# Half of a layer's first matrix product by Strassen's scheme, in a fused windowed-attention and MLP kernel

## The chip, the cores and the metric

The kernel runs on one core of one Trainium2 chip. The metric is device time in microseconds (us), the median over several runs; lower is better. The core has five engines that run beside each other, each with an in-order queue of its own: TensorE (PE in the profile; PEld is its weight load), VectorE (DVE), ScalarE (ACT), GpSimd (POOL) and SyncE (SP), which here only issues DMAs.

## The reference

Attention over a window with four sink positions, then a layer norm and an MLP with a residual. The draw gives 4 batches, 8 heads, 768 positions, head size 64, so 3072 rows of 512 columns go into the MLP, whose hidden width is 2048.

```python
scores = scale * q @ k.T                      # per batch and head, scale = 1/sqrt(64)
keep = (pos_k < 4) | ((pos_q - pos_k >= 0) & (pos_q - pos_k < 128))
a = softmax(where(keep, scores, -1e9))
x = (a @ v).transpose(0, 2, 1, 3).reshape(B, S, H * D)
xn = (x - mean(x)) / sqrt(var(x) + 1e-6) * g_ln
out = x + maximum(xn @ w_ch1, 0.0) @ w_ch2    # w_ch1: 512x2048, w_ch2: 2048x512
```

## The kernel before

**Tiling.** The 3072 rows are 12 chunks (`NC`) of 256 rows, three to a batch; `c` is the chunk, `R = c % 3` its place in the batch. A chunk has two tiles `t` of 128 rows. For each chunk `chunk` loads q, k and v (DMAs from GpSimd's queue: `nat`, `vn`) and transposes q and k (DMA transposes from SP's queue: `kq`); `attend` makes the scores (TensorE into a pair of PSUM banks, L763, with the sinks of L767), their exponentials (ScalarE, L777, bf16 `pe`), and multiplies these by a band mask (VectorE, L781); `value` multiplies by v (TensorE, L800 for the sinks, L805), divides by the sums and takes the layer norm's statistics (VectorE, L818 to L826), the inverse root (GpSimd, L832 and L833), the normed rows (VectorE, L835) and transposes them by a DMA into `xnt` (L845).

**First layer.** `mlp` computes, for a chunk, 16 column groups of 128 hidden values, two to a step `u` of eight: per step 8 matmuls of 128x128 weights by 256 rows of `xnt` into one PSUM bank `ph` (L880), then a relu into `hq` (L890 on ScalarE or L892 on VectorE). For the first two chunks the matmuls stream 128 rows instead (L873).

**Second layer.** From the third chunk on, `wino` computes it with Winograd's form of Strassen's scheme: four sums of parts of the hidden values (`s1` to `s4`, VectorE, L943, `hs`), then seven products of eight matmuls (`p1`, `p2`, `p7`, `p6`, `p4`, `p5`, `p3`, L960), and VectorE instructions that combine PSUM regions and the residual (`keep`, L974; `final`, L981).

**Order.** Nothing is left to the hardware's choice: each step is an `op` with the engines that may run it, an assumed duration and a priority; `Plan.run` lays them out in a list schedule, and every engine's queue is emitted in the order of the planned starts. From priority 40 on TensorE's order is that of the priorities alone. With `T = 16c + 8`, the first layer of chunk `c` has priorities `T + 0.5 + u`, and the seven products follow 8 later; the scores of the next chunk have priority `T - 5.3` and `T - 2.0`, its value products `T + 2` and `T + 3`. Buffers come from rings: four single PSUM banks (`one`), two pairs (`pair`), 8 `hq`, 10 `hs`, 16 `x`, 12 `pe`.

Of the kernel before, what the change touches and what calls it, by code (L numbers as in the profile page):

```python
# [7 lines left out]
FP32 = mybir.dt.float32  # L8
BF16 = mybir.dt.bfloat16
# [55 lines left out]
class Plan:  # L65
# [7 lines left out]
    SHARED = 36.0  # L73

# [38 lines left out]
    def run(self):  # L113
# [8 lines left out]
        while ready:  # L122
# [50 lines left out]
            if o.dma is None:  # L173
                o.end = st + lat
            else:
                busy, first, last = o.dma
                q = "POOL" if e == "POOL" else "HW"
                at = max(st + occ + first, dma_free[q], dma_free["all"] if st < self.SHARED else 0.0) + busy
                dma_free[q] = dma_free["all"] = at
                o.end = at + last  # L180
                lanes[q][n_dma[q] % self.LANES] = o.end
                n_dma[q] += 1
# [29 lines left out]
def fix(occ, extra=0.09):  # L212
# [11 lines left out]

LOW, HIGH = 1e-9, 1e9
# [4 lines left out]
           w1p=(0.15, 1.7, 2.05, 2.8), pm=2, w2p=(4.5, 4.51, 4.52, 4.53), by_tile=2, wino=2, vp=(0.0, 0.1, 2.0, 2.1, 4.2, 4.3), ld1=0.05)  # L230
# [131 lines left out]
def kernel(  # L362
# [47 lines left out]
    ring("pe", 12, [128, 2, 512], BF16)  # L410
    ring("ps", 3, [128, 256], BF16)
    ring("kts", 2, [128, HP, 32], BF16)
    ring("x", 16, [128, DM], BF16)
# [3 lines left out]
    ring("hs", 10, [128, 2, 2, 128], BF16)  # L417
    ring("tm", 6, [128, 256], FP32)
# [101 lines left out]
    for b in range(1, B):  # L520
        P.op(f"vs{b}", {"DVE": dve(520)}, 48.0 * b - 20, lambda e, b=b: V.tensor_tensor(
            vs[b], vc[:, b, :].unsqueeze(1).to_broadcast([128, H, 65]),
            sel.unsqueeze(2).to_broadcast([128, H, 65]), op=ALU.mult),
            reads=[Bc["vcd"], Bc["vc"], Bc["sel"]], writes=[Bvs[b]], nb=40.0 * b)
# [11 lines left out]
    def at(c, step):  # L536
        return 16.0 * c - 8.0 + PAR[step]
# [17 lines left out]
    def behind(c):  # L555
        return [roots[2 * (c - 3) + 1]] if c >= PAR["behind"] else []

    def load_v(t, prio):
        b, r = t // RB, t % RB
        bv = Buf(f"v{t}", "vn")  # L560
        vn_b[t] = bv
        P.op(f"vld{t}", {"POOL": (0.87, 0.9)}, prio, lambda e: G.dma_start(  # L562
            bv.t[:, :, 0:64], v[b, :, 128 * r:128 * (r + 1), :].rearrange("h p d -> p h d")),
            writes=[bv], dma=SW, after=list(ones_of.values()) + behind(t // 2))
# [13 lines left out]
    def chunk(c):  # L578
# [54 lines left out]
        elif c < PAR["by_dma"]:  # L633
            loaded = Buf(f"l{c}")
            for i in range(2):
                load4(c, "kq"[i], (PAR["ld1"] if c == 1 else ld) + 0.01 * i, loaded)
            for hh in range(2):
                pt = Buf(f"pt{c}{hh}", "one")

                def tr(e, pt=pt, hh=hh):  # L640
                    pb = pt.t.bitcast(BF16).rearrange("p (h k i g) -> p h i k g", h=2, k=2, i=4)
                    for h in range(2):
                        for i in range(4):
                            for h2 in range(2):
                                nc.tensor.transpose(pb[64 * h2:64 * h2 + 64, h, i], n4_b[c].t[:, 4 * hh + 2 * h + h2, i, :], ident)  # L645
                P.op(f"tr{c}{hh}", pe(0.46), d + 0.02 + 0.1 * hh, tr, reads=[loaded, Bc["ident"]],
                                  hold=[n4_b[c], T], writes=[pt], mode="c")
                done = Buf(f"T{c}{hh}")
                tile_of[2 * c, hh] = tile_of[2 * c + 1, hh] = done
                evict(f"ev{c}{hh}", d + 0.05 + 0.1 * hh, 1024,  # L650
                      lambda pt=pt: pt.t.bitcast(BF16).rearrange("p (m i g) -> p m g i", m=4, i=4),
                      lambda hh=hh: T.t[:, 2 * hh:2 * hh + 2].rearrange("p h k (g i) -> p (h k) g i", i=4), [pt], [T, done], fp=True)
        else:
            for x, (nm, src) in enumerate((("k", k), ("q", q))):
                for i in range(2):
                    nat = Buf(f"{nm}n{c}{i}", "nat")
                    ap = src[b, :, 256 * R + 128 * i:256 * R + 128 * (i + 1), :].rearrange("h p d -> p h d")
                    P.op(f"{nm}ld{c}{i}", {"POOL": (0.87, 0.9)}, ld + 0.01 * i + 0.1 * x,
                         lambda e, nat=nat, ap=ap: G.dma_start(nat.t, ap), writes=[nat], dma=SW, after=behind(c))  # L659
                    P.op(f"tr{nm}{c}{i}", {"SP": (1.2, 1.2)}, d + 0.01 * i, lambda e, nat=nat, i=i, x=x: dma_t(  # L660
                        T.t[:, :, x, 128 * i:128 * i + 128], nat.t.rearrange("p h d -> p (h d)")),
                        reads=[nat], writes=[T], dma=HW_X, after=[scores[c - 1]])
# [75 lines left out]
    def attend(c):  # L738
# [6 lines left out]
        for half in range(2):  # L745
# [28 lines left out]
            for j, pp in enumerate(pps):  # L774
# [5 lines left out]
                P.op(f"mk{c}{hp}", {"DVE": dve(2 * n, 0.52)}, d + 0.2 + 0.05 * j, lambda e, pb=pb, mm=mm:  # L780
                     V.tensor_mul(pb.t[:, :, 0:n], pb.t[:, :, 0:n], mm),  # L781
                     reads=[Bc["mask" if R else "mask0"]], rw=[pb])
# [4 lines left out]
        for i in range(2):  # L787
# [3 lines left out]
            value(c, i, pes, ps, (PAR["av2"] if c == 2 else at(c, "av")) + PAR["avi"] * i, part, [2 * c + i - 1, 2 * c + i] if R or i else [2 * c])  # L791

    def value(c, i, pes, ps, d, part, srcs):
# [24 lines left out]
        P.op(f"rc{t}", {"DVE": fix(0.115)}, d + 0.1, lambda e: V.reciprocal(rc(), pv()[:, :, :, 64]),  # L818
             reads=[po], writes=[rcb])
        P.op(f"x{t}", {"DVE": dve(512)}, d + 0.11, lambda e: V.tensor_tensor(  # L820
# [3 lines left out]
        P.op(f"bn{t}", {"DVE": fix(0.60)}, d + 0.12, lambda e: V.bn_stats(st.t[:, 8:14], x.t),  # L824
             reads=[x], writes=[st, mv])
        P.op(f"ag{t}", {"DVE": fix(0.09)}, d + 0.13, lambda e: V.bn_aggr(st.t[:, 14:16], st.t[:, 8:14]),  # L826
# [4 lines left out]
        roots[t] = P.op(f"rs{t}", {"POOL": (0.83, 0.88)}, d + (0.5 if scaled else 5), lambda e: (  # L831
# [3 lines left out]
        P.op(f"xc{t}", {"DVE": fix(0.26)}, d + (0.6 if scaled else 0.14), lambda e: V.tensor_scalar(  # L835
# [8 lines left out]
        if c >= PAR["x_by_dma"]:  # L844
            P.op(f"trx{t}", {"SP": (1.2, 1.2)}, d + 0.5, lambda e: dma_t(xnt_b[c].t[:, :, 128 * i:128 * i + 128], xc.t),  # L845
                 reads=[xc], writes=[xnt_b[c]], dma=HW_X)
# [13 lines left out]

    def mlp(c):
# [5 lines left out]
        for u in range(NH1 // 2):  # L867
# [15 lines left out]
            pr = T + u + 0.5  # L883
# [9 lines left out]
            P.op(f"rl{c}_{u}", {"ACT": act(512), "DVE": dve(512)}, pr - 3, rl, reads=[ph], writes=[hb], hold=[hg])  # L893
            h1.append(hb)
        T += 8
        if c >= PAR["wino"]:
            return wino(c, T, hq, h1)
# [29 lines left out]
    def wino(c, T, hq, h1):  # L927
# [3 lines left out]
        deps = {n: [h1[4 * g + (0 if n[2] == "1" else 1)::2][:2] for g in range(2)] for n in part}  # L931
# [7 lines left out]
        for i, (n, x0, x1, op) in enumerate((("s3", "a11", "a21", ALU.subtract), ("s1", "a21", "a22", ALU.add),  # L939
                                             ("s2", "s1", "a11", ALU.subtract), ("s4", "a12", "s2", ALU.subtract))):  # L940
            for g in range(2):
                sb[n, g] = Buf(f"{n}_{c}{g}", "hs")
                P.op(f"{n}_{c}{g}", {"DVE": dve(512, 0.52)}, T - 4 + 4 * g + 0.2 * i, lambda e, n=n, x0=x0, x1=x1, g=g, op=op: V.tensor_tensor(  # L943
# [27 lines left out]
        def keep(name, r, done, half, pr):  # L971
            tm[name] = Buf(f"tm{name}{c}", "tm")
            i, sl = half // 2, slice(256 * (half % 2), 256 * (half % 2) + 256)
            return P.op(f"tm{name}_{c}", {"DVE": dve(256, 1.14)}, pr, lambda e: V.tensor_tensor(  # L974
# [3 lines left out]
        def final(r, done, name, half, pr):  # L978
            i, sl = half // 2, slice(256 * (half % 2), 256 * (half % 2) + 256)
            oo[half] = Buf(f"oo{c}{half}")  # L980
            return P.op(f"o{c}_{half}", {"DVE": dve(256, 1.14)}, pr, lambda e: V.tensor_tensor(  # L981
# [51 lines left out]
    for c in range(NC):  # L1033
        mlp(c)
# [94 lines left out]
```

## Time and profile before

| what | value |
|---|---|
| median of 3 runs | 211.38 us (210.68 to 211.71) |
| the profiled execution's own time | 211.71 us |
| its span, first to last instruction | 210.2 us |
| TensorE busy | 203.0 us, 97% |
| VectorE busy | 162.2 us, 77% |
| ScalarE busy | 114.1 us, 54% |
| GpSimd busy | 83.5 us, 40% |
| granted TensorE clock | 1.000 |

Durations in a row are of one instruction; TensorE's instructions overlap, so the pace of a stream of matmuls is read from the time a run of them takes in the chain of waits, divided by their number, and not from the mean of one. Engines that are not on the chain may idle at no cost.

### The profile page before, as it was taken

To read this page: it belongs to the slowest core of one execution; us is meant where nothing else is said; L and a number is where in the kernel's file an instruction comes from. 1 tells how busy PE (TensorE), PEld (TensorE's weight loads), DVE (VectorE), ACT (ScalarE), POOL (GpSimd) and SP (SyncE) were. 2 spreads that over 40 slices of the span, in tenths; PEclk is the share of its full clock that TensorE was granted. 3 is DMA by queue.
4 is the path that set the end of the run, shared out by engine and by line. 5 is a ranking of instruction groups with operands and counts; after the bars stand their busy time and mean duration, and the time that the engine had idled before them with its cause. 6 is when DMAs were issued, how large, how long until landed. Compare 5 with 4: busy or idle time off the path is not lost.

```text
span 210.2 us, 6259 instructions
## 1 busy us (share of the span) xinstructions
PE 203.0 (97%) x2539; PEld 167.9 (80%) x2544; DVE 162.2 (77%) x410; ACT 114.1 (54%) x168; POOL 83.5 (40%) x126
## 2 busy tenths in 40 slices
PE   6978999999999999999999999999999999999994
PEld 2657997764787997997987987987988988988883
DVE  5579759999688688798687797797787786797353
ACT  2559479837564564564556555554457457450620
POOL 7967583369058057058066066066020020020000
PEclk9999999999999999999999999999999999999999
DMA  5999999999999949939959939939954520220202
GB/s 115 156 198 191 199 191 208 189 173 154 212 167 127 172 109 136 188 78 120 166 122 150 174 79 156 172 77 151 177 100 53 150 53 3 100 50 4 103 30 83
DMA packets 101243, 27.51 MB, mean 131 GB/s; under 512 B 89556, under 2 KB 99032, under 8 KB 101208
## 3 DMA queue, kind: packets, MB, share of 16 engines
q0 software_dynamic: 67712, 13.37, 77.7%
q1 hardware_dynamic: 33208, 13.41, 35.5%
q8 instruction: 21, 0.34, 0.7%
q10 hardware_dynamic: 288, 0.26, 0.4%
q14 instruction: 14, 0.11, 0.2%
HBM read 27.30 MB, written 6.29 MB: 160 GB/s over the span
## 4 chain that ended last, share of the span: by engine, by line
PE 90%; DMA 3%; DVE 3%; POOL 2%; issue 0%; DVEq 0%
PE one L880 33%; PE one L960 30%; PE one L873 7%; PE one L911 7%; PE pair L805 5%; PE pair L763 4%; DMA n4b<-in_q_dram 3%; PE pair L800 2%; PE one L645 1%; POOL nat L599 1%; PE one L767 1%; DVE xnt L857 1%; DVE kq L568 1%; POOL vn L562 0%; DVE st L824 0%
## 5 line engine op out<-in xcount | busy, mean ns | idle before, releaser
L890 ACT ACTIVATE hq<-one 128x512 bf16<-128x512 f32 x92 | 55.0, 597 | 55.7 <-PE one L880 46.7
L880 PE MATMUL one<-xnt,w 128*128 128x256 bf16 x640 | 74.5, 273 | 0.0
L880 PEld LDWEIGHTS <-w 128*128 128x128 bf16 x640 | 61.4, 98 | 7.0
L777 ACT ACTIVATE pe<-pair 128x1024 bf16<-128x1024 f32 (+1 forms) x40 | 36.2, 960 | 23.2 <-PE pair L763 19.0
L832 POOL TENSOR_SCALAR st<-st 128x1 f32<-128x1 f32 x24 | 6.2, 259 | 88.2 <-DVE rec L818 74.6
L960 PEld LDWEIGHTS <-hs 128*128 128x128 bf16 x320 | 30.0, 98 | 5.2 <-DVE tm L974 0.3
L974 DVE TENSOR_TENSOR tm<-one,x 128x256 f32<-128x256 f32 x40 | 16.9, 422 | 12.3 <-PE one L960 12.3
L781 DVE TENSOR_TENSOR pe<-pe,mask 128x1024 bf16<-128x1024 bf16 (+1 forms) x40 | 24.9, 644 | 1.0 <-ACT pe L777 0.8
L960 PEld LDWEIGHTS <-hq 128*128 128x128 bf16 x240 | 23.5, 98 | 2.7
L562 POOL DMA_DIRECT2D vn<-in_v_dram x24 | 21.8, 922 | 2.0 <-DMA w<-in_moe_w_ch_dram 1.1
L943 DVE TENSOR_TENSOR hs<-hq 128x512 bf16<-128x512 bf16 x40 | 15.4, 413 | 5.3 <-ACT hq L890 5.2
L960 PE MATMUL one<-w,hq 128*128 128x256 bf16 x160 | 19.1, 273 | 0.0
L981 DVE TENSOR_TENSOR ot<-one,tm 128x256 f32<-128x256 f32 x40 | 16.7, 418 | 1.1 <-PE one L960 0.9
L820 DVE TENSOR_TENSOR x<-pair,rec 128x512 bf16<-128x512 f32 x24 | 16.6, 691 | 0.8
L824 DVE BATCH_NORM_STATS2 st<-x 128x6 f32<-128x512 bf16 x24 | 16.6, 692 | 0.5
L873 PE MATMUL one<-xnt,w 128*128 128x128 bf16 x256 | 16.3, 219 | 0.5 <-DVE xnt L857 0.5
L873 PEld LDWEIGHTS <-w 128*128 128x128 bf16 x256 | 14.7, 98 | 1.6 <-issue 0.5
L659 POOL DMA_DIRECT2D nat<-in_k_dram x16 | 15.0, 938 | 2.5 <-DMA w<-in_moe_w_ch_dram 2.5
L659 POOL DMA_DIRECT2D nat<-in_q_dram x16 | 14.2, 898 | 3.4 <-DMA w<-in_moe_w_ch_dram 3.4
L833 POOL TENSOR_TENSOR st<-st,mhalf 128x1 f32<-128x1 f32 x24 | 14.2, 592 | 2.0
L911 PE MATMUL one<-w,hq 128*128 128x512 bf16 x60 | 14.8, 380 | 0.2
L805 PE MATMUL pair<-vn,pe 128*128 128x65 bf16 x352 | 14.6, 193 | 0.0
(113 smaller groups left out, 245.1 us busy)
## 6 DMA issues: line engine op xcount, KB each, us to landing
out_dram<-ot SPq DMA_DIRECT2D x17, 256.0 KB
w<-in_moe_w_ch_dram POOLq DMA_DIRECT2D x8, 512.0 KB, 12.6
vn<-in_v_dram POOLq DMA_DIRECT2D x24, 128.0 KB, 7.2
nat<-in_k_dram POOLq DMA_DIRECT2D x17, 128.0 KB, 4.8
nat<-in_q_dram POOLq DMA_DIRECT2D x17, 128.0 KB, 5.3
out_dram<-ot SPq DMA_DIRECT2D x14, 128.0 KB
kq<-nat SPq DMA_TRANSPOSE x32
xnt<-xc SPq DMA_TRANSPOSE x20
```

Source lines behind the costliest of these rows:

```text
L562: P.op(f"vld{t}", {"POOL": (0.87, 0.9)}, prio, lambda e: G.dma_start(bv.t[:, :, 0:64], v[b, :, 128 * r:128 * (r + 1), :].rearrange("h p d ...
L659: lambda e, nat=nat, ap=ap: G.dma_start(nat.t, ap), writes=[nat], dma=SW, after=behind(c))
L777: P.op(f"ex{c}{hp}", {"ACT": act(2 * n)}, d + 0.1 + 0.05 * j, lambda e, pp=pp, pb=pb: nc.scalar.activation(pb.t[:, :, 0:n], pp.t[:, :, 0:n ...
L781: V.tensor_mul(pb.t[:, :, 0:n], pb.t[:, :, 0:n], mm),
L805: nc.tensor.matmul(po.t[:, h // 4, 65 * (h % 4):65 * (h % 4) + 65], lhsT=part(h, n), rhs=vn_b[tv].t[:, h, :], start=(not R and h % 4 == 0 ...
L873: nc.tensor.matmul(ph.t[:, 128 * s:128 * s + 128], lhsT=w1[u // 2][:, j, 128 * s:128 * s + 128], rhs=xnt.t[:, j, 128 * (u % 2):128 * (u % ...
L880: nc.tensor.matmul(ph.t[:, 256 * s:256 * s + 256], lhsT=w1[ht // 4][:, j, 128 * (ht % 4):128 * (ht % 4 + 1)], rhs=xnt.t[:, j, :], start=j ...
L890: nc.scalar.activation(hg.t[:, u % 4, :], ph.t, AF.Relu)
L911: nc.tensor.matmul(pc.t[:, 0:wd], lhsT=(hq[s // 2].t[:, (2 * s + i) % 4, 128 * ii:128 * ii + 128] if by_tile else hq[ht // 8].t[:, ht // 2 ...
L960: nc.tensor.matmul(at(r), lhsT=get(left, g)[:, v, s, :], rhs=rhs, start=first and n == 0, stop=n == 7, skip_group_check=True)
L974: return P.op(f"tm{name}_{c}", {"DVE": dve(256, 1.14)}, pr, lambda e: V.tensor_tensor(tm[name].t, at(r), xs[i].t[:, sl], op=ALU.add), read ...
L981: return P.op(f"o{c}_{half}", {"DVE": dve(256, 1.14)}, pr, lambda e: V.tensor_tensor(ots[i].t[:, sl], at(r), tm[name].t, op=ALU.add), read ...
```

## The change

From the fifth chunk on (`c >= 4`, eight chunks) the first 1024 of the 2048 hidden columns are computed by `halves` in place of steps `u` = 0 to 3. The 512x1024 weights and the 256 rows are each split two by two, and seven products of half the size in every dimension replace eight: each is 8 matmuls that stream 128 rows. Products 1, 6, 7 and 4 add up in one PSUM bank `z`, products 5 and 3 in `y`, and product 2 has `w`. Between products ScalarE copies the partial sums that are needed elsewhere to SBUF (`tz`, 128x512 f32: after products 1, 5 and 6); VectorE adds a bank and such a copy into `hq` (three `total`s, 128x512), ScalarE applies the relu to these in place, and for the fourth block straight from the bank. GpSimd makes four differences of the row blocks (`xt`, 128x256 bf16 each) per chunk; VectorE makes four sums of weight parts (128x1024 bf16) once, in buffers of `hq`'s ring.

Besides: steps 4 to 7 keep their eight matmuls, in the order 5, 6, 4, 7; their relus are planned on ScalarE only (but in the last chunk). From chunk 5 on the first of a chunk's four band masks (where `R` is not 0) is made by GpSimd with two `affine_select`s. The sink values of batches 2 and 3 (L521) are made on GpSimd. Priorities of chunks 5 to 11 get a set of their own (`PAR["h"]`), the sums `s1` to `s4` and `keep` and `final` other ones; rings `pe` and `x` shrink to 10 and 12. Other hunks add figures to the planner: a longer assumed landing of DMAs, and a model of mixed DMA queues which a start time of 1e9 (`MIXED`) keeps from use.

```diff
 PAR = dict(...
+           h=dict(av=0.85, avi=-0.0, sc=-7.68, sc1=-2.94, tr=-24.25, trx=9.0, xo=-13.3), mkp=(0,), mko=-3.93, vsp=1, soon=0, lb=0, xlag=2.1, llag=2.4, ..., tzp=20.19, kp=-0.95, half=4, wsum=58.0, flip=1, te=("POOL",), tlead=58.56, rd=0, cpr=15.35, sp=(10.27, 4.87), sq=(-1.16, -17.0, 5.05, 17.16), pos=(-1.36, 0.58, 4.21, 6.8, 1.47, 1.55, 4.55), pos4=(4.77, 3.73, 4.73, 5.69))
...
-    ring("pe", 12, [128, 2, 512], BF16)
+    ring("pe", 10, [128, 2, 512], BF16)
...
-    ring("x", 16, [128, DM], BF16)
+    ring("x", 12, [128, DM], BF16)
...
+    ring("xt", 2, [128, 4, 2, 128], BF16)
+    ring("tz", 2, [128, 512], FP32)
...
-        P.op(f"vs{b}", {"DVE": dve(520)}, 48.0 * b - 20, lambda e, b=b: V.tensor_tensor(
+        P.op(f"vs{b}", {"DVE": dve(520)} if b == 1 or not PAR["vsp"] else {"POOL": (1.3, 1.4)}, 48.0 * b - 20, lambda e, b=b: (V if e == "DVE" else G).tensor_tensor(
...
+                if R and c > PAR["half"] and hp in PAR["mkp"]:
+                    def band(e, pb=pb):
+                        for u in range(2):
+                            v = pb.t.rearrange("p a (b u c) -> p (a b) u c", u=2, c=128)[:, :, u, :]
+                            G.affine_select(out=v, in_=v, compare_op=(ALU.is_gt, ALU.is_ge)[u], fill=0.0, base=0,
+                                            pattern=[[0, 4], [2 * u - 1, 128]], channel_multiplier=1 - 2 * u)
+                    P.op(f"mk{c}{hp}", {"POOL": (1.45, 1.55)}, d + PAR["mko"] + 0.05 * j, band, rw=[pb])
...
+    def halves(c, T, hq):
...
+        for i, (n, x0, x1) in enumerate((("t0", "b12", "b11"), ("t2", "b22", "b12"), ("t1", "b22", "t0"), ("t3", "b21", "t1"))):
+            got[n] = Buf(f"x{n}_{c}")
+            last_xt = P.op(f"xt{n}_{c}", {e: dve(256, 0.52) if e == "DVE" else fix(0.72) for e in PAR["te"]}, T - PAR["tlead"] + 0.1 * i, lambda e, n=n, x0=x0, x1=x1: (V if e == "DVE" else G).tensor_tensor(
+                right(n), right(x0), right(x1), op=ALU.subtract), reads=[xnt] + [got[x] for x in (x0, x1) if x[0] == "t"],
+                hold=[sums], writes=[got[n]])
...
+            def mm(e):
+                lt = a[left]() if isinstance(left, str) else wsum[left][0]()
+                rh = right(rt)
+                for h in range(4):
+                    for kk in range(2):
+                        nc.tensor.matmul(b.t[:, 128 * h:128 * h + 128], lhsT=lt[:, kk, 128 * h:128 * h + 128], rhs=rh[:, kk, :],
+                                         start=first and h == 0 and kk == 0, stop=kk == 1, skip_group_check=True)
...
+        m1 = product(1, "z", "a11", "b11", True)
+        t1, o1 = snap(1, "z", m1)
+        m5 = product(5, "y", 0, "t0", True)
+        t5, o5 = snap(5, "y", m5)
+        m2 = product(2, "w", "a12", "b21", True)
+        total("c11", "w", m2, t1, T + pos[1] - late_)
+        m6 = product(6, "z", 1, "t1", False, [o1])
+        t2, o2 = snap(6, "z", m6)
+        m3 = product(3, "y", 3, "b22", False, [o5])
+        total("c12", "y", m3, t2, T + pos[5] - late_)
+        m7 = product(7, "z", 2, "t2", False, [o2])
+        o3 = total("c22", "z", m7, t5, T + pos[6] - late_)
+        m4 = product(4, "z", "a22", "t3", False, [o3])
+        outs["c21"] = Buf(f"c21_{c}")
+        P.op(f"rc21_{c}", {"ACT": act(512)}, T + pos[3] - PAR["tzp"], lambda e: nc.scalar.activation(
+            block("c21"), banks_["z"].t.rearrange("p (i t) -> p i t", i=4), AF.Relu), reads=[m4], hold=[banks_["z"], hq], writes=[outs["c21"]])
...
-        for u in range(NH1 // 2):
+        strassen = c >= PAR["half"]
+        quick = halves(c, T, hq[0]) if strassen else None
+        for u in range(4 if strassen else 0, NH1 // 2):
...
-            P.op(f"rl{c}_{u}", {"ACT": act(512), "DVE": dve(512)}, pr - 3, rl, reads=[ph], writes=[hb], hold=[hg])
+            P.op(f"rl{c}_{u}", {"ACT": act(512)} if strassen and c < NC - 1 else {"ACT": act(512), "DVE": dve(512)}, pr - 3, rl, reads=[ph], writes=[hb], hold=[hg])
```

139 lines of the change are left out of this document (111 added, 28 removed).

## The prediction

> **What bounds the kernel now.** First the page's busy shares, the slices and the shares of the chain that ended last.
>
> ```profile
> span 210.2 us, 6259 instructions
> PE 203.0 (97%) x2539; PEld 167.9 (80%) x2544; DVE 162.2 (77%) x410; ACT 114.1 (54%) x168; POOL 83.5 (40%) x126
> ...
> PE   6978999999999999999999999999999999999994
> ...
> DVE  5579759999688688798687797797787786797353
> ...
> PEclk9999999999999999999999999999999999999999
> ...
> PE 90%; DMA 3%; DVE 3%; POOL 2%; issue 0%; DVEq 0%
> ```
>
> TensorE is busy in every slice from the fourth on, at the full granted clock, and makes 90% of the chain. Next the chain of waits in order of time (start, length, what), to see whether that busy time has holes in it, and at what pace each kind of matmul goes.
>
> ```profile
> 21.64 0.89 PE one L873 x16
> ...
> 24.58 3.72 PE one L873 x64
> ...
> 30.43 1.89 PE one L873 x32
> ...
> 119.02 0.87 PE one L880 x8
> 119.89 0.22 PE pair L800 x2
> 120.12 0.48 PE pair L805 x16
> 120.60 4.37 PE one L880 x40
> 124.97 1.75 PE one L960 x16
> 126.71 0.46 PE pair L763 x24
> 127.17 0.22 PE one L767 x4
> 127.40 2.73 PE one L960 x24
> 130.12 0.46 PE pair L763 x24
> 130.59 1.85 PE one L960 x16
> 132.44 1.75 PE one L880 x16
> ...
> 193.75 7.09 PE one L880 x64
> 200.84 6.13 PE one L960 x56
> ```
>
> Each piece begins where the one before it ended, so in the steady part nothing but TensorE's own work sets the time: what is taken from its stream comes off the end, until another engine makes it wait. A matmul that streams 256 rows takes 4.37/40 = 109.2 ns. One that streams 128 rows takes 0.89/16 = 55.6 ns, 3.72/64 = 58.1 ns or 1.89/32 = 59.1 ns, each with a weight load of its own in front of it. Last, how much room the other engines have in the chunk before the change begins and in three later ones that follow each other (stretch, length, then busy time of PE, PEld, DVE, ACT, POOL).
>
> ```profile
> 73.22:89.09 15.87, 15.87 (x210) 13.79 (x209) 12.86 (x32) 8.93 (x13) 7.02 (x10) 1.00 1.39 149
> 103.37:119.89 16.52, 16.52 (x216) 14.34 (x215) 13.05 (x32) 9.31 (x14) 7.02 (x10) 1.00 1.39 152
> 119.89:135.77 15.88, 15.88 (x211) 13.78 (x209) 12.96 (x32) 8.93 (x13) 7.02 (x10) 1.00 1.49 138
> 135.77:150.05 14.28, 14.28 (x156) 12.26 (x155) 11.85 (x31) 7.37 (x12) 7.03 (x10) 1.00 1.34 124
> ```
>
> In the 46.68 us of the last three rows VectorE works 13.05 + 12.96 + 11.85 = 37.86 us, so 8.8 us are free. ScalarE and GpSimd are far from full. VectorE is the engine that could become the next bound.
>
> **TensorE's part of the change.** Per chunk, steps 0 to 3 are 4 x 8 = 32 matmuls of 256 rows, 32 x 109.2 = 3.49 us. In their place stand 7 x 8 = 56 matmuls of 128 rows: 3.11 us at 55.6 ns, 3.25 us at 58.1 ns, 3.31 us at 59.1 ns. The products come eight at a time between other work, which is nearest to the short run of 16, but the dearer rows hold long runs; I take 57 ns, 3.19 us, so 0.30 us less per chunk. Eight chunks give 2.4 us, with ends of 1.4 and 3.0 us.
>
> Here a rule speaks against the change. The Trainium skill, "TensorE: Matmul & The Clock Gate", section Back-to-back issue gap, gives about 81 ns as the sustained pace of pairs of weight load and 128-row matmul. By it the products would take 56 x 81 = 4.54 us, 1.05 us more per chunk. This trace has just such pairs, and the row of 64 of them at 58.1 ns disagrees.
>
> **What TensorE must wait for.** The seven products share banks with copies in between. By the priorities the order around a chunk is: m1, p3 of the chunk before, m2, the two value products of the next chunk, m5, m6, step 5, m3, m7, steps 6, 4, 7, m4, then the next scores and p1. A copy or relu from a bank is 597 ns, a full product 8 x 109 = 0.87 us, a half one 0.45 us.
>
> ```profile
> L890 ACT ACTIVATE hq<-one 128x512 bf16<-128x512 f32 x92 | 55.0, 597 | 55.7 <-PE one L880 46.7 <-PE one L873 8.6 <-DVE st L826 0.4
> L873 PE MATMUL one<-xnt,w 128*128 128x128 bf16 x256 | 16.3, 219 | 0.5 <-DVE xnt L857 0.5
> L820 DVE TENSOR_TENSOR x<-pair,rec 128x512 bf16<-128x512 f32 x24 | 16.6, 691 | 0.8
> L781 DVE TENSOR_TENSOR pe<-pe,mask 128x1024 bf16<-128x1024 bf16 x28 | 18.5, 683 | 0.5 <-ACT pe L777 0.5
> L943 DVE TENSOR_TENSOR hs<-hq 128x512 bf16<-128x512 bf16 x40 | 15.4, 413 | 5.3 <-ACT hq L890 5.2
> L521 DVE TENSOR_TENSOR vs<-vc,sel 128x520 bf16<-128x520 f32 x3 | 2.1, 693 | 0.0
> L833 POOL TENSOR_TENSOR st<-st,mhalf 128x1 f32<-128x1 f32 x24 | 14.2, 592 | 2.0
> L832 POOL TENSOR_SCALAR st<-st 128x1 f32<-128x1 f32 x24 | 6.2, 259 | 88.2 <-DVE rec L818 74.6 <-DVE st L826 13.3
> L463 POOL TENSOR_SCALAR_AFFINE_SELECT upper<-upper 128x128 bf16<-128x128 bf16 x1 | 0.3, 294 | 0.0
> ```
>
> A half product's result stands 0.16 us after its last slot (219 ns for one, 57 in the stream). So m3 needs m5's copy, 0.16 + 0.60 = 0.76 us after m5, and is due 0.45 + 0.87 = 1.32 us after it. m7 needs the copy of m6, which waits on ScalarE for the copy of m5: at the latest 0.76 + 0.60 = 1.36 us after m5, and due at 1.32 + 0.45 = 1.77. m4 needs VectorE's sum of m7, 0.16 + 0.69 = 0.85 us, and has three full products, 2.6 us. All of it fits, with 0.4 us to spare at the tightest place. The second layer's p7 needs the relu after m4 and then a sum on VectorE, 0.16 + 0.60 + 0.41 = 1.17 us, and has p1 and p2, 1.75 us, in front of it. In the last chunk, where no scores stand between, that is the same room. So the direct waits cost nothing; what can cost is the queue in front of them: ScalarE's copies stand behind relus that wait for VectorE's sums, and one that starts 0.7 us late would leave 0.3 us on TensorE. That would be in part of the chunks: bounds are 0 and 0.3 us in all eight, 2.4 us; I take a fifth, 0.5 us, since the 0.4 us of room at the tightest place holds two thirds of a relu that got in front.
>
> **VectorE.** Added: three sums of 128x512 with a PSUM operand and bf16 out, 0.69 each by the L820 row, 2.07 us per chunk. Gone: a band mask (0.68) in two chunks of three, and one sink value (0.69) in the three above. Over three chunks that is 37.86 + 6.2 - 1.4 - 0.7 = 42.0 us of 46.68 - 0.9 = 45.8 us, 92%. It still fits, with 3.8 us free. The weight sums are four once, 128x1024 like a mask, 4 x 0.68 = 2.7 us, and lie in the chunks before the fifth, where the stretch from 73.22 has 15.87 - 12.86 = 3.0 us free; with that cover gone they would cost up to 2.7 us.
>
> **ScalarE and GpSimd.** ScalarE goes from 8 evictions per chunk to 11: 3 x 0.60 = 1.8 us on 8.93, 10.7 of 15.6 us. GpSimd gets four differences of 128x256 a chunk, two selects of 128x512 in two chunks of three, and two sink values. No row shows these. From below: 259 ns for one element and 294 for 128 give 0.27 ns an element, so 0.33 us for 256 and 0.40 for 512. From above: the two-input 592 ns for one element and VectorE's unpacked 691/512 = 1.35 ns an element give 0.94 and 1.3 us. In the middle, 0.6 and 0.8 us, a chunk's six take 4.0 us; at the upper end 6.4 us. With the 7.02 us of now that is 11 to 13.4 of 15.6 us: it fits. GpSimd now waits for the DMA transposes that give `xnt`, and for the exponentials that it masks; queued behind these waits are its DMA issues for later chunks and the layer norm's roots, for which VectorE's normed rows wait:
>
> ```profile
> L835 DVE TENSOR_SCALAR xc<-x,st 128x512 bf16<-128x512 bf16 x24 | 10.0, 415 | 4.4 <-POOL st L833 4.2
> ...
> 124.28 0.41 DVE L835 TENSOR_SCALAR xc<-x,st 128x512 bf16<-128x512 bf16 x1
> ```
>
> These waits sum to 4.2 us already. Four middle-sized differences in front of a root would add 2.4 us to one; the rows normed at 124.28 are first used at 132.44 (the L880 piece above), 8 us later, so that is covered and costs nothing on TensorE, unless VectorE has no room left.
>
> **The sum.** 211.71 us for the profiled execution (1.5 us of it outside the span) less 2.4 plus 0.5 is 209.8 us. The median of the runs is 0.33 us below the profiled one, so the forecast is **209.5 us**.
>
> **Rivals.** *GpSimd's new work holds up VectorE.* Per three chunks there are 12 differences and 4 selects, 16 instructions that read SBUF at length. If each delays VectorE by d, its 3.8 us are gone at d = 0.24 us, and the whole gain of 0.9 us at 4.7/16 = 0.29 us. VectorE spends 24 sums x 0.41 + 10 masks x 0.68 = 16.6 of its 42.0 us on instructions with two SBUF operands. If such a one is put off until GpSimd's instruction ends, d is about half of that: 0.33 us by the middle sizes (mean 0.65), 0.52 by the upper ones (1.03). Since VectorE has one-operand work in between, I stay near the lower, 0.36: 16 x 0.36 - 3.8 = 2.0 us of delay in three chunks, 4.6 us in the seven that overlap with attention. Then 211.4 - 2.4 + 4.6 gives 213.6 us, slower. Overlaps of the kind are short in this trace:
>
> ```profile
> 123.65 0.60 POOL L833 TENSOR_TENSOR st<-st,mhalf 128x1 f32<-128x1 f32 x1
> ...
> 123.85 0.42 DVE L943 TENSOR_TENSOR hs<-hs,hq 128x512 bf16<-128x512 bf16 x1
> ```
>
> A two-operand sum starts in the middle of GpSimd's two-operand instruction and takes its usual 0.42 us. That speaks against it, but with one element per partition the GpSimd instruction may hardly have touched the memory. The Trainium skill, "SBUF — State Buffer", section Who interferes with whom, states that a VectorE instruction with two SBUF inputs and a GpSimd instruction that reads SBUF shut each other out for the whole instruction. These two rows do not show that; no row has a longer GpSimd read to try it on.
>
> *Queues hand on delays.* VectorE at 92% puts the three sums late, the relus behind them hold up ScalarE's copies, and m7 or m3 waits in each chunk. At 0.3 us a chunk the gain of 2.4 us is eaten: 211.4 us, no change. At 0.6 us a chunk, 213.8 us, slower; that needs a copy 1 us late, the length of an exponential in front of it.
>
> *The 128-row pace is 81 ns.* 8 x 1.05 = 8.4 us more, 219.8 us. The rows of L873 leave little room for it.
>
> **How the numbers follow.** A measurement of this kernel can tell about 0.5%, 1.06 us, from no change. The forecast has 0.55 (its own range 208.3, all of 3.0 us and no wait, to 210.3). GpSimd holding up VectorE has 0.21, delays in the queues 0.23, of which 0.15 end within 0.5% and 0.08 slower, the 81 ns 0.01. So faster 0.55, the same 0.15, slower 0.30. The range goes from 208.3 to 213.6 us, which takes in the first rival's price and leaves out its dearer forms.
>
> **What would show it.** Right: the chain after goes on without holes, eight 128-row matmuls take 0.45 to 0.47 us, a period of a chunk is 0.2 to 0.35 us shorter, VectorE is about 92% busy in the middle chunks, sums of L943 keep 0.41 us. Wrong: pieces of VectorE, ScalarE or GpSimd in the chain between the fifth and the last chunk; two-operand VectorE rows whose mean grows by a tenth of a us or more; TensorE waiting for the copies or for `xt`; a half product of 0.65 us would be the pace rule.

## The result, and the profile after

The changed kernel takes 209.96 us (median of 20 runs, 208.54 to 211.82) against 211.38 us (20 runs, 210.68 to 212.40): a ratio of 0.9927, with a 95% interval of 0.9910 to 0.9945. Ratios, here and below, are taken from fast runs alone (the run of 211.82 us is a slow one), so they differ a little from the quotients of the medians. It is faster by 0.7%, more than the 0.5% that the prediction took for the least that can be told apart, and 0.5 us slower than the forecast of 209.5 us. Its profiled execution took 209.80 us, 1.91 less than that of before.

The page of after: span, busy times, VectorE's slices, the shares of the chain.

```profile
span 208.3 us, 6722 instructions
PE 200.6 (96%) x2736; PEld 168.1 (81%) x2736; DVE 177.7 (85%) x433; ACT 122.3 (59%) x190; POOL 117.0 (56%) x170
...
DVE  6579767999699898898879989989989979997783
...
PE 85%; DMA 9%; POOL 3%; issue 1%; DVE 0%; SPq 0%
```

TensorE is busy 2.4 us less, and is still the bound. VectorE's slices have filled up to 8 and 9, and DMAs now have 9% of the chain, where they had 3%. The chain in order of time says which transfers these are (start, length, what; a load of the start-up, the first product of the third chunk, the first half products of a later one, and the last piece of TensorE's products):

```profile
9.30 13.70 DMA w<-in_moe_w_ch_dram
...
55.16 1.75 PE one L1011 x16
...
95.92 5.03 DMA xnt<-xc
...
101.00 0.61 PE one L942 x8
...
102.48 0.45 PE one L942 x8
...
103.67 0.89 PE one L942 x16
...
199.00 6.13 PE one L1093 x56
```

Of the 208.3 us, 13.70 are a load of weights at the start of the program; before, the chain went by another load there, of 7.32 us. That says nothing of the change. The other transfer, 5.03 us, is new. Sixteen matmuls of the half products take 0.89 us, eight 0.45: 55.6 to 56 ns for one of 128 rows. But at 101.00 the chain leaves TensorE: the first half product `m1` has waited for the transposes of the normed rows, 5.03 us long. TensorE's own list of waits gives how long (total, times, longest):

```profile
PE one L668 <- DMA n4b<-in_q_dram: 1.4, 1, 1.4
...
PE one L942 <- DMA xnt<-xc: 0.4, 1, 0.4
```

The stretch of three steady chunks (length, then busy time of PE, PEld, DVE, ACT, POOL), and in it the VectorE instructions with two operands in SBUF, the on-chip memory, grouped by shape; under these, the shorter masks of the same three chunks before:

```profile
103.67:149.30 45.63, 45.63 (x651) 40.58 (x649) 42.15 (x100) 29.19 (x47) 34.59 (x48) 1.00 1.40 140
```

```profile
L814 DVE TENSOR_TENSOR pe<-pe,mask 128x1024 bf16<-128x1024 bf16 x6 | 5.3, 914 | 0.0
...
L1076 DVE TENSOR_TENSOR hs<-hs,hq 128x512 bf16<-128x512 bf16 x6 | 3.8, 635 | 0.0
L814 DVE TENSOR_TENSOR pe<-pe,mask 128x768 bf16<-128x768 bf16 x4 | 2.5, 670 | 0.0
...
L1076 DVE TENSOR_TENSOR hs<-hq,hs 128x512 bf16<-128x512 bf16 x6 | 2.2, 413 | 0.0
```

```profile
L781 DVE TENSOR_TENSOR pe<-pe,mask 128x768 bf16<-128x768 bf16 x4 | 2.1, 550 | 0.0
```

Three chunks take 45.63 us where they took 46.68, 0.35 us less each, and TensorE has no hole in them. Of the grouped rows one keeps its length, `hs<-hq,hs` with 0.41 us; the masks went from 683 to 914 ns and from 550 to 670, `hs<-hs,hq` from 0.42 to 0.64 us. GpSimd's and VectorE's new instructions over the whole run:

```profile
L922 POOL TENSOR_TENSOR xt<-xnt 128x256 bf16<-128x256 bf16 x16 | 13.4, 855 | 8.9 <-DMA xnt<-xc 8.9
L922 POOL TENSOR_TENSOR xt<-xnt,xt 128x256 bf16<-128x256 bf16 x16 | 12.0, 750 | 0.6
L809 POOL TENSOR_SCALAR_AFFINE_SELECT pe<-pe 128x512 bf16<-128x512 bf16 x10 | 7.2, 744 | 4.2 <-ACT pe L802 4.2
L964 DVE TENSOR_TENSOR hq<-one,tz 128x512 bf16<-128x512 f32 x24 | 16.1, 674 | 0.7 <-PE one L942 0.4
```

**Where VectorE's instructions grow.** The growth of the means is that of a few instructions, and these grow by much. The sums `hs<-hs,hq` have a median of 418 ns and a longest of 1612 (the three numbers behind the first colon are least, median and longest). GpSimd's and VectorE's instructions of one chunk, side by side, say which:

```profile
L1076 DVE TENSOR_TENSOR hs<-hs,hq x20: 415/418/1612, 60.7 to 201.1; 128x512 bf16<-128x512 bf16 x20
```

```profile
111.98 1.75 POOL L809 TENSOR_SCALAR_AFFINE_SELECT pe<-pe 128x512 bf16<-128x512 bf16 x2
...
114.99 1.74 POOL L922 TENSOR_TENSOR xt<-xnt 128x256 bf16<-128x256 bf16 x2 [0.39 <-DMA xnt<-xc]
```

```profile
112.11 1.12 DVE L814 TENSOR_TENSOR pe<-pe,mask 128x1024 bf16<-128x1024 bf16 x1
...
114.15 0.75 DVE L1076 TENSOR_TENSOR hs<-hq,hs 128x512 bf16<-128x512 bf16 x2
```

The mask at 112.11 stands beside two selects and takes 1.12 us in place of 0.68. The two sums at 114.15 end at 114.90, just before the differences begin, and take 0.75 us together, 0.41 each. It is so in the whole trace: of 119 masks and sums from those of L814 and L1076, 92 meet none of GpSimd's differences and selects in time, and none of these 92 is more than 10 ns over its usual 683, 552 or 417 ns; the 27 that meet one are longer by 0.29 us on average, by 1.2 at most. GpSimd's pay too: the 11 differences that meet none of these VectorE instructions take 0.66 to 0.70 us, the other 21 up to 1.17.

**Where the time went.** TensorE's last product ends at 199.00 + 6.13 = 205.13 us, before at 200.84 + 6.13 = 206.97: 1.84 us earlier. The half products save 3.49 - 56 x 0.0558 = 0.37 us a chunk, 2.9 us in eight. Start-up came 0.47 us later in this execution (the first product of the third chunk starts at 55.16 us, before at 54.69; the wait for `n4b` above, 1.4 us in place of 1.2, and one of 0.2 for weights are part of it). The hole at 101.00 costs 0.4 of wait and 0.16 of a slow first piece (0.61 for 0.45 us). -2.9 + 0.47 + 0.56 = -1.87 us: for the two profiled executions that is all of it. The medians are 1.42 us apart and not 1.91; the difference lies in executions that left no trace.

### The profile page after: what moved, and what is told of

It reads as the page before. It is cut to its first block, busy times and chain, and to the rows that moved or that the text cites. A ratio compares the mean times of both kernels' runs of the same rounds, so it can differ in the third digit from the quotient of the medians.

```text
span 208.3 us, 6722 instructions
## 1 busy us (share of the span) xinstructions
PE 200.6 (96%) x2736; PEld 168.1 (81%) x2736; DVE 177.7 (85%) x433; ACT 122.3 (59%) x190; POOL 117.0 (56%) x170
## 4 chain that ended last, share of the span: by engine, by line
PE 85%; DMA 9%; POOL 3%; issue 1%; DVE 0%; SPq 0%
PE one L1093 28%; PE one L1011 20%; PE one L942 12%; PE one L1042 7%; DMA w<-in_moe_w_ch_dram 7%; PE one L1004 5%; PE pair L838 5%; PE pair L788 4%; DMA xnt<-xc 2%; PE pair L833 2%; PE one L668 1%; POOL nat L622 1%; POOL vn L585 1%; PE one L792 1%; POOL w L543 1%; POOL n4b L598 1%
## 5 line engine op out<-in xcount | busy, mean ns | idle before, releaser
L1011 PE MATMUL one<-xnt,w 128*128 128x256 bf16 x384 | 45.5, 273 | 0.0
L1021 ACT ACTIVATE hq<-one 128x512 bf16<-128x512 f32 x58 | 34.1, 594 | 19.4 <-PE one L1011 9.6
L1011 PEld LDWEIGHTS <-w 128*128 128x128 bf16 x384 | 36.6, 98 | 4.1
L1093 PEld LDWEIGHTS <-hs 128*128 128x128 bf16 x320 | 30.6, 98 | 3.9 <-DVE hs L1076 0.2
L967 ACT ACTIVATE hq<-hq 128x512 bf16<-128x512 bf16 x24 | 15.1, 628 | 19.7 <-DVE hq L964 19.7
L814 DVE TENSOR_TENSOR pe<-pe,mask 128x1024 bf16<-128x1024 bf16 (+1 forms) x35 | 25.5, 757 | 0.9 <-ACT pe L802 0.8
L1093 PEld LDWEIGHTS <-hq 128*128 128x128 bf16 x240 | 22.3, 98 | 4.1 <-issue 0.3
L953 ACT COPY tz<-one 128x512 f32<-128x512 f32 x24 | 13.3, 583 | 12.5 <-PE one L942 12.3
L1093 PE MATMUL one<-w,hq 128*128 128x256 bf16 x160 | 19.2, 273 | 0.0
L922 POOL TENSOR_TENSOR xt<-xnt 128x256 bf16<-128x256 bf16 x16 | 13.4, 855 | 8.9 <-DMA xnt<-xc 8.9
L1076 DVE TENSOR_TENSOR hs<-hq 128x512 bf16<-128x512 bf16 x40 | 15.7, 421 | 2.5 <-ACT hq L1021 1.9
L964 DVE TENSOR_TENSOR hq<-one,tz 128x512 bf16<-128x512 f32 x24 | 16.1, 674 | 0.7 <-PE one L942 0.4
L1004 PEld LDWEIGHTS <-w 128*128 128x128 bf16 x256 | 14.7, 98 | 2.0 <-issue 0.5
```

The costliest lines, as they stand in the source:

```text
L1004: nc.tensor.matmul(ph.t[:, 128 * s:128 * s + 128], lhsT=w1[u // 2][:, j, 128 * s:128 * s + 128], rhs=xnt.t[:, j, 128 * (u % 2):128 * (u % ...
L1011: nc.tensor.matmul(ph.t[:, 256 * s:256 * s + 256], lhsT=w1[ht // 4][:, j, 128 * (ht % 4):128 * (ht % 4 + 1)], rhs=xnt.t[:, j, :], start=j ...
L1021: nc.scalar.activation(hg.t[:, u % 4, :], ph.t, AF.Relu)
L1093: nc.tensor.matmul(at(r), lhsT=get(left, g)[:, v, s, :], rhs=rhs, start=first and n == 0, stop=n == 7, skip_group_check=True)
```

## The experiments

Four theories were set against each other. A: TensorE's saving comes through, and VectorE stays off the path. B: GpSimd's reads lengthen VectorE's instructions, and that is what limits the gain. C: the landing of `xnt` at `m1` is what is late. D: it is VectorE's load itself. Ratios are to the kernel before, with 95% intervals; each edit is to the changed kernel.

Two things must be known first. One is the end of the program. The last two matmuls of the program (L1190) and the last wait of SP's queue, in after and in e2 (window at the end of each):

```profile
205.63 0.19 PE L1190 MATMUL one<-ones_f,ot 128*1 128x1 f32 x2 [0.52 <-DVE ot L1114]
```

```profile
205.85 0.19 PE L1190 MATMUL one<-ones_f,ot 128*1 128x1 f32 x2 [0.52 <-DVE ot L1114]
...
SPq L1259 <- DVEq L1224: 1.9, 1, 1.9
```

The spans end at 208.3 and 210.3: from the last matmul it is 2.7 us in after, and 4.4 in e2, where SP waits 1.9 us for VectorE's sequencer at the end of the program. It is 2.6 to 2.7 us in before, after, e4, e5, e6, e8, e9 and e11, and 4.3 to 4.5 in e1, e2, e3, e7, e10 and e12. The eight traces with the short end have 408 to 433 VectorE instructions, the six with the long one 435 to 472: it goes with the program, so it is likely to sit in each of its executions, though only one of each was traced. Why it happens was not tried. These 1.7 us are no work of the kernel, and are called the tail.

The other is the start: the third chunk begins up to 1.5 us earlier in one trace than in another. Both are left out by the time from the first matmul of the third chunk (L1011, before L880) to the end of the last product (L1093, before L960), called the middle here:

| trace | middle, us |
|---|---|
| before; e8, no product | 152.4; 152.8 |
| after; e9, the same kernel again | 150.1; 149.7 |
| e5, `m1` later | 149.5 |
| e10, `m1` later, mask on VectorE | 150.0 |
| e2, mask on VectorE | 151.5 |
| e7, differences on VectorE, late; e1, early | 150.9; 165.6 |

Each is one execution; the two of the same kernel are 0.4 us apart, the size of after's wait at `m1`.

**e1, the differences on VectorE.**

```diff
-te=("POOL",)
+te=("DVE",)
```

> The kernel after with the four differences of the row blocks on VectorE in place of GpSimd; masks and sink values stay on GpSimd. Theory A (TensorE's saving of 0.36 us a chunk comes through; VectorE, though lengthened by GpSimd's reads, is off the path): VectorE gets 4 x about 0.25 us a chunk, and its masks and sums with two SBUF operands fall back from means of 0.84 and 0.50 us towards 0.68 and 0.42; these nearly cancel, the time stays within 0.5 us of 210.0. Theory B (GpSimd's reads hold VectorE up so far that TensorE loses by it, which is why 1.4 us came of the 2.9 us in the stream): faster than after by about 1 us, 209.0.

Measured: 225.6 us, 1.061 (1.057 to 1.065), the worst but one. TensorE's waits, VectorE's wait for the transposes with the group it belongs to, two stretches of 5 us (busy time of PE, PEld, DVE, ACT, POOL, then the granted clock), and a piece of the chain in the first of them:

```profile
PE one L1093 <- DVE hs L1076: 6.3, 6, 1.8
PE one L1093 <- DVE tm L1107: 5.5, 3, 3.1
...
DVE xt L922 <- DMA xnt<-xc: 4.7, 3, 3.1
...
L922 DVE TENSOR_TENSOR xt<-xnt,xt 128x256 bf16<-128x256 bf16 x16 | 4.6, 288 | 0.3
```

```profile
100.00:105.00 5.00, 3.72 (x26) 2.86 (x26) 3.32 (x10) 0.59 (x1) 0.00 (x0) 0.66 1.71 155
...
155.00:160.00 5.00, 4.08 (x32) 3.22 (x32) 3.25 (x9) 0.59 (x1) 0.00 (x0) 0.66 0.97 166
```

```profile
103.17 1.89 PE one L1093 x8
```

A difference takes 0.29 us on VectorE, a third of GpSimd's 0.75 to 0.86. What costs is where it stands: at the head of an in-order queue, waiting up to 3.1 us for the transposes, with the second layer's sums behind it. Between the profiled executions (225.94 and 209.80) lie 16.1 us: 11.8 are these waits, 1.7 the tail, and 2 x (1.89 - 0.87) = 2.0 the lower clock, where eight matmuls of 256 rows took 1.89 us in place of 0.87, once in each of the two stretches. The other 0.6 us were not traced one by one: each wait has a slow first piece behind it, as the hole in after had, and the start came 1.1 us earlier than in after.

**e2, the band mask on VectorE.**

```diff
-mkp=(0,)
+mkp=()
```

> The kernel after with the first band mask back on VectorE. Theory A: VectorE gets 0.68 us in two chunks of three and loses some waits for GpSimd's selects; no change within 0.5 us. Theory B: slower by up to 1 us if VectorE's load binds, faster by up to 1 us if GpSimd's reads do.

Measured: 211.45 us, 0.999 (0.998 to 1.001). Less the tail that is 209.7 us, as after. But the middle of its trace is 1.4 us longer than after's. The largest of TensorE's new waits there is C's again; two more are 0.5 us for a load of v and 0.2 for VectorE's mask.

```profile
PE one L942 <- DMA xnt<-xc: 1.0, 1, 1.0
```

So the medians show no gain from GpSimd's ten selects, and the one trace a loss of 1.4 us without them, most of it at `m1`; e10 takes this up. One thing it settles: with the selects gone and the differences still on GpSimd, `hs<-hs,hq` is back at a mean of 417 ns (after: 494, and 437 in e9), while the masks still have 820 (after: 842). These sums grow beside the selects; the masks grow beside either (in e1, with the selects alone, they have 775).

**e3, differences, mask and sink values on VectorE.**

```diff
-mkp=(0,), vsp=1, te=("POOL",)
+mkp=(), vsp=0, te=("DVE",)
```

> The kernel after with differences, masks and sink values all on VectorE, as if nothing had been moved to GpSimd. Theory A: VectorE's load is near what it is now (1.0 + 0.45 us of work a chunk more, about 1 us of waits less), the time within 0.5 us of 210.0, and rows with two SBUF operands at 0.68 and 0.42 us as before. Theory B, load: VectorE over its room, slower than after by 1 to 3 us. Theory B, reads: faster by 1 us or more.

Measured: 228.71 us, 1.077 (1.072 to 1.083). The order of e1 again, and more of it: TensorE waits 9.2 us for the sums `hs` where e1 had 6.3. Its use is the price of VectorE's instructions when GpSimd reads nothing at length:

```profile
L814 DVE TENSOR_TENSOR pe<-pe,mask 128x1024 bf16<-128x1024 bf16 x28 | 18.1, 683 | 0.5 <-ACT pe L802 0.5
L1076 DVE TENSOR_TENSOR hs<-hs,hq 128x512 bf16<-128x512 bf16 x20 | 8.3, 417 | 0.0
```

683 and 417 ns, as before the change: the lengthening in after comes of the work that was moved to GpSimd.

**e4, each difference on GpSimd twice** (the second writes the same again).

```diff
-                right(n), right(x0), right(x1), op=ALU.subtract)
+                right(n), right(x0), right(x1), op=ALU.subtract) for _ in range(2)]
```

> The kernel after with each of GpSimd's four differences a chunk made twice (the second writes the same values again), in the same planned order; VectorE's own work is unchanged. It doubles GpSimd's reads alone. Theory A: VectorE's rows with two SBUF operands lengthen again by what they did, about 2.4 us in three chunks, which its free 3.5 us just hold; GpSimd goes from 34.6 to about 44 of 45.6 us in three chunks; 0 to 1 us slower than after. Theory B: VectorE has no room now, so every lengthening comes out on TensorE: 4 to 6 us slower.

Measured: 214.68 us, 1.015 (1.012 to 1.018). Waits, and the mask's row:

```profile
PE one L942 <- POOL xt L922: 3.1, 3, 1.6
...
PE one L1093 <- DVE hs L1076: 0.9, 3, 0.3
...
L814 DVE TENSOR_TENSOR pe<-pe,mask 128x1024 bf16<-128x1024 bf16 x23 | 20.3, 908 | 0.5 <-ACT pe L802 0.5
```

That is 4.7 us over after: A was wrong, which put 0 to 1 us on it, and B, which put 4 to 6, was right by its number alone. TensorE waits for GpSimd's differences (3.1 us) and for the transposes (1.1), less for VectorE (0.9), and 32 more reads raise the mask from 842 ns to 908 only, where the same kernel as after had 874 in e9. The largest part is GpSimd's own chain, from the landing to the products that need it, which has no room for four more instructions.

**e5, `m1` later**: one of the seven positions in TensorE's order is moved, to behind product `p3` of the chunk before.

```diff
-pos=(-1.36, 0.58,
+pos=(0.2, 0.58,
```

> The kernel after with product m1 behind p3 of the chunk before in TensorE's order, in place of ahead of it: m1 is due one full product, 0.87 us, later. Theory C (what is lost of the 2.9 us is TensorE waiting at m1 for the DMA transposes of the normed rows, which land 5 to 6 us after VectorE made them, beside six loads of 128 KB): the hole of 0.6 us goes, 0.3 to 0.8 us faster than after, about 209.4, and the runs lie closer together. Theory D (VectorE's load itself makes the loss, as the 1.5 us that the mask cost suggest): the order of m1 changes nothing, 210.0.

Measured: 208.90 us, 0.989 (0.986 to 0.993), the fastest of all. The whole list of TensorE's waits:

```profile
PE pair L1220 <- DVE vn L487: 1.8, 1, 1.8
PE one L668 <- DMA n4b<-in_q_dram: 1.2, 1, 1.2
PE one L1004 <- DVE xnt L891: 0.5, 1, 0.5
PE one L1190 <- DVE ot L1114: 0.5, 1, 0.5
PE pair L738 <- DVE x L854: 0.3, 1, 0.3
```

All five are of the start and the end, and stand in before's list too: from the fifth chunk to the last product TensorE waits for nothing. That alone would not show C, since the same kernel as after, in e9, has no such wait either. What shows it is where the landing lies, by GpSimd's first difference, which it releases, and `m1`, the first eight of the sixteen:

```profile
145.31 1.45 POOL L922 TENSOR_TENSOR xt<-xnt 128x256 bf16<-128x256 bf16 x2 [1.28 <-DMA xnt<-xc]
```

```profile
145.96 0.89 PE one L942 x16
```

In its old place, 0.87 us earlier, `m1` would have been due at 145.09, before the landing. In an earlier chunk it is the same: the difference at 99.95, `m1` at 100.38, in its old place at 99.51. So C holds for this trace: the move took two waits of some tenths of a us away. In the median e5 is 1.06 us below after and 0.65 below e9, but the intervals of the ratios overlap.

**e6, loads held until the differences are done.**

```diff
-lb=0
+lb=1
```

> The kernel after with the switch that holds the loads of q, k and v of a later chunk back until GpSimd's differences are made, so that the DMA transposes of the normed rows meet few loads. Theory C: the transposes land about 2 us earlier, no hole at m1, 0.3 to 0.8 us faster than after, unless the loads now come late for the next scores. Theory D: no change, 210.0.

Measured: 213.58 us, 1.009 (1.006 to 1.012). GpSimd's queue now stands 21.8 us at the head of the differences, and layer norm's roots and the loads stand behind it. TensorE waits 2.9 us for the sums `hs` and 1.2 for transposed q and k:

```profile
POOL xt L922 <- DMA xnt<-xc: 21.8, 6, 6.1
...
DVE xc L869 <- POOL st L867: 8.5, 11, 2.3
```

Did the transposes land earlier? From the issue of a chunk's second transpose to GpSimd's first difference, the four chunks behind the first take 5.0, 3.7, 4.5 and 5.3 us here, and 5.2, 4.9, 5.3 and 5.7 in after. That is earlier by 0.1 to 1.2 us, less than the 2 us expected, and TensorE has no wait at `m1`; what the held loads delay costs more. After's last chunk shows the transposes with no load of q, k or v beside them, as GpSimd issues none later than 150 us (the second transpose, and the difference that waits for both):

```profile
186.72 1.22 SPq L565 DMA_TRANSPOSE xnt<-xc  x1
```

```profile
189.33 1.53 POOL L922 TENSOR_TENSOR xt<-xnt 128x256 bf16<-128x256 bf16 x2 [3.92 <-DMA xnt<-xc]
```

2.6 us in place of 4.9 to 5.7: this fits loads that make the transposes slow. It is not shown, as the last chunk differs in other transfers too, and no run left the loads out.

**e7, the differences on VectorE, but late in its order.**

```diff
-xlag=2.1, te=("POOL",), tlead=58.56
+xlag=5.5, te=("DVE",), tlead=10.0
```

> The differences on VectorE as in e1, but placed late in its queue, behind the chunk's masks and most of the sums that the second layer needs (their priority is lowered and the planner's landing time of the transposes is set to 5.5 us). VectorE's work is the same as in e1. If the 14 us of e1 were its order (a wait for a DMA at the head of VectorE's queue, with work behind it for which TensorE waits): back to 209.5 to 212. If they were VectorE's load: 220 us or more.

Measured: 211.65 us, 1.001 (0.999 to 1.004); less the tail 209.9, as after. The same 32 instructions on the same engine cost 14 us less than in e1 (14.7 in the middle). So e1's 14 us are its order and not VectorE's load. The middle is still 0.8 us longer than after's, with waits of 0.8 us at `m1`.

**e8, no Strassen product.** By the same figure the band masks, the relus and the priorities of later chunks are as before; the rings, the sink values on GpSimd, the other priorities and the planner's figures are the changed kernel's.

```diff
-half=4
+half=99
```

> The kernel after without Strassen in the first layer in any chunk: no products, copies, differences, weight sums, no masks on GpSimd and not the second set of priorities; what stays are the smaller rings, the new priorities of the sums of the second layer, and two sink values on GpSimd. If those are neutral, as the prediction took them: 211.4, as before, within 0.5 us. If they bring part of the gain: under 210.9; if they cost part of it: over 211.9.

Measured: 211.75 us, 1.001 (0.999 to 1.004). What is left of the change is neutral; the gain belongs to the products and what is switched with them. The masks on GpSimd are not needed for it: e10 has none, and a middle of 150.0 us.

**e9, the changed kernel again**, for the spread.

> The kernel after, unchanged, on the chip of the next three runs, so that these can be set against it: 210.0 within 0.5 us, with runs spread over 2 us or more, and a wait of TensorE at m1 for the DMA transposes in its profile.

Measured: 209.55 us, 0.991 (0.987 to 0.994). Its profiled execution (span 207.6 us) has no wait at `m1`, so the hole is not in every run. Of what was expected the median came, but not the wait, nor a spread of 2 us: the six times lie within 1.0 us. In one chunk of the trace `m1` starts at 145.92 us and GpSimd's first difference at 146.02, as close together as at after's hole (101.00 and 101.09), so there the landing came just in time. After's 20 times have a standard deviation of 0.72 us, before's 20 one of 0.41: a hole that comes and goes fits this, but of the two traces of this kernel one has it.

**e10, `m1` later and the mask on VectorE.**

```diff
-mkp=(0,), pos=(-1.36, 0.58,
+mkp=(), pos=(0.2, 0.58,
```

> As e5, m1 behind p3, and as e2 the first band mask back on VectorE. Theory C (the 1.5 us that e2 lost were the normed rows coming later on VectorE, so the transposes later, so m1 later): with m1 due 0.87 us later most of them are covered, within 0.6 us of e5, 208.9 to 209.5. Theory D (VectorE's load itself): again 1.5 us above e5, 210.4.

Measured: 210.93 us, 0.997 (0.995 to 1.000). As measured that is nearer to D's 210.4; less a tail of 1.6 us it is 209.3, what C gave. The traces decide it: the middle is 150.0 us, 0.4 over e5's and 1.5 under e2's, which differs from this kernel in the place of `m1` alone. TensorE does not wait at `m1`; its only wait of over 0.2 us that e5 has not is one of 0.6 us for a load of v. So most of what e2's trace lost was C's wait, and VectorE has the room for the masks.

**e11, `m1` and `m2` behind the value products.**

```diff
-pos=(-1.36, 0.58,
+pos=(0.9, 1.0,
```

> The kernel after with both m1 and m2 behind the next chunk's value products: m1 is due 2.7 us later than in after, but only m2 and m5, 0.9 us, lie between m1 and m6, which needs the copy of m1, 0.76 us at least. If room for the transposes is still short in e5: faster than e5 by up to 0.3 us. If the copy is now late: slower than e5 by 0.1 to 0.5 us a chunk, 209.7 to 213. Theory C with e5 having room enough: the first does not show.

Measured: 211.67 us, 1.000 (0.997 to 1.002). Too far: VectorE's sums and outputs come too late for what follows.

```profile
PE one L1093 <- DVE ot L1114: 1.4, 2, 1.1
```

**e12, `m1` later, and the product in nine chunks in place of eight.**

```diff
-half=4, wsum=58.0, pos=(-1.36, 0.58,
+half=3, wsum=42.0, pos=(0.2, 0.58,
```

> As e5, with Strassen from the fourth chunk on instead of the fifth (nine chunks; the weight sums are planned 16 us earlier). If a chunk's 0.36 us in TensorE's stream is all there is: 0.36 us faster than e5, 208.5. If VectorE's room before the fifth chunk, 3 us a chunk of which the weight sums take 2.7, is gone by then: same as e5 or slower by up to 2 us.

Measured: 212.00 us, 1.003 (1.000 to 1.005); less the tail of 1.6 us 210.4, still 1.5 above e5, though one more chunk should save 0.37. `hs<-hq,hs` has grown to 645 ns (e5: 519), and TensorE waits for VectorE:

```profile
PE one L1093 <- DVE ot L1114: 1.2, 1, 1.2
...
L1076 DVE TENSOR_TENSOR hs<-hq,hs 128x512 bf16<-128x512 bf16 x20 | 12.4, 645 | 0.0
```

## Why the prediction was right, step by step

- **TensorE's saving: right, a little small.** 57 ns a matmul were taken, 55.8 measured; 2.4 us forecast, 2.9 measured, inside the bounds of 1.4 to 3.0. The row with 16 matmuls was the nearest, as the text said; going part of the way to the dearer rows gave 0.5 us away. The rule of the Trainium skill, "TensorE: Matmul & The Clock Gate", section Back-to-back issue gap, which would have made a loss of it with 81 ns a pair, is contradicted by 448 more matmuls. e8 and e10 leave no other part that could have brought the gain but the relus and the priorities of later chunks, and TensorE's account above has no room for more.
- **Waits in the banks' copies: the place was wrong, the size agrees by luck.** 0.5 us were put on ScalarE's copies holding up m3 or m7. No such wait is in the list of after. 0.56 us stand at `m1` in this execution, and none in e9's, and `m1` the text had covered: "rows normed at 124.28 are first used at 132.44 ... 8 us later, so that is covered". This step failed. It set the 8 us against 2.4 us of GpSimd's differences and left out the rows' own way: issue and landing of the transposes take 5 us (5.03 at the hole, 4.9 to 5.7 in the chunks around it), and the new order puts `m1` ahead of `p3`. In the steady chunks the landing is 0.3 to 1.0 us ahead of `m1`: in one of them GpSimd's first difference, which the landing releases, starts at 146.49 us and `m1`, by the chain, at 146.79:

```profile
146.49 1.83 POOL L922 TENSOR_TENSOR xt<-xnt 128x256 bf16<-128x256 bf16 x2 [1.24 <-DMA xnt<-xc]
...
146.79 0.45 PE one L942 x8
```

  e5, and e10 against e2, move this one product, and no wait is left.
- **The sum: right by luck in its last tenths.** 211.71 - 2.4 + 0.5 gave 209.8 us for the profiled execution, and 209.80 was measured. But TensorE saved 0.5 us more than was put down, and the start-up, of which the sum has no term, came 0.47 us later.
- **VectorE's 42.0 of 45.8 us: measured 42.15 of 45.63, by two errors that cancel.** A sum was 674 ns, as the 0.69 taken. But the two-operand rows of the three chunks have grown by 6 x 0.23 + 6 x 0.22 + 4 x 0.12 = 3.2 us, which the sum did not hold. Against it stands that neighbouring instructions overlap: the lengths of all VectorE's instructions in the stretch add up to 42.2 us before and 48.6 after, 6.4 more where the sum had 4.1, but they cover 37.86 and 42.15 us, so that the overlap has grown by 2.1.
- **GpSimd's prices: inside the bounds.** 0.75 to 0.86 us a difference on average (0.6 taken, bounds 0.33 to 0.94; 0.66 to 0.70 where none of VectorE's two-operand instructions is beside it), 0.74 a select (0.8 taken). 11.5 us a chunk (34.59/3) is in the 11 to 13.4.
- **The rival of GpSimd holding up VectorE: the mechanism is there, the size did not reach.** Those 3.2 us over 12 differences and 4 selects are d = 0.20 us. The rival took 0.36; VectorE was to be full at 0.24. By this reckoning 0.6 of its 3.8 us stayed free; by the trace 45.63 - 42.15 = 3.5 us did, as the lengthened instructions overlap more. One of the signs that the text gave for being wrong, two-operand rows longer by a tenth of a us, came true, without a wait of TensorE for VectorE in after's middle. e12 shows VectorE late when more is asked of it. The two short rows quoted against the rival were no evidence, as the text suspected. The rule of the Trainium skill, "SBUF — State Buffer", section Who interferes with whom, is borne out: such VectorE instructions grow only where they meet GpSimd's reads in time (27 of 119 do; in e3, without these reads, none), and `hs<-hq,hs` kept 413 ns in the middle chunks because none of its six met one. What kept the price under the rival's is that few meet, and that GpSimd's instruction is often the one that waits, up to 1.17 us in place of 0.66.
- **The rival of handed-on delays: not in after**; e11 is what it may look like, at 1.7 us above after.
- **What was called free** (the weight sums, the relus on ScalarE, the rings, the priorities): e8, with what does not hang on the product, is 1.001 of before, with 1 in the interval. The weight sums, the relus and the priorities of later chunks were not tried alone; no wait for them is in the list.

## What to carry to other kernels

When work moves earlier in an engine's order, follow its input back through the DMA that brings it: the landing, here 5 us, counts against the slack, and the row that shows the slack of before is not that of after. A cheap instruction that waits for a DMA is best put where the least stands behind it: differences of 0.29 us at the head of VectorE's queue cost 14 us more than the same ones late in its order, and those of 0.75 to 0.86 us on GpSimd made TensorE wait nowhere. When a mean has grown, look at the median and the longest: here most instructions kept their length, and the few that grew met another engine's. Before a difference of 1 us is explained, see how long the end of the program took in each.

## What was not expected of the hardware

- The tail: 4.3 to 4.5 us in place of 2.7 from the last matmul to the end of the span, with SP waiting 1.8 to 2.0 us for VectorE's sequencer, in six of the twelve experiments. Less it, the medians of e2, e7 and e10 are at after's or below. The cause is open.
- In e1 the granted clock fell to 0.66 in two stretches of 5 us, behind holes in TensorE's work of 2.0 and 3.1 us. e3, with holes of 2.2 and 3.0 us, had no such stretch in the middle of its run; what sets it off is open.
- GpSimd's lengthening of VectorE does not go with the number of its reads, but with how many meet in time: of the 119 instructions 27 met one in after, and 30 in e4 with 32 more reads, where the mask's mean rose by 66 ns on top of the 159 of after.
